# A fused cosine attention and mixer kernel: the second token mixing of odd batches cut into other bunches, one weight cast moved, the last matmul group halved

## The chip, the core and the metric

The kernel runs on one core of a Trainium2 chip. The core has five engines with their own instruction queues: TensorE (PE in the profile; PEld is its weight loading), VectorE (DVE), ScalarE (ACT), GpSimd (POOL) and SyncE (SP, which here only issues transfers). The engines work in parallel and wait for each other through semaphores. Inside one queue the order is fixed: an instruction that waits holds up everything behind it. The metric is the device time of one execution in microseconds (us), given as the median of several runs. Lower is better.

## The reference

Eight batches of twelve attention heads, each 448 positions by 64, feed a mixer block. With the names of the reference:

```python
q_n = q / (norm(q) + 1e-06);  k_n = k / (norm(k) + 1e-06)
scores = q_n @ k_n.T / tau                     # tau = 0.1
attn = softmax(scores);  x = attn @ v          # heads side by side: x is 448 x 768 for each batch
h = relu(x.T @ w_tok1) @ w_tok2                # token mixing: 448 -> 256 -> 448
u = x + h.T
h2 = relu(u @ w_ch1) @ w_ch2                   # channel mixing: 768 -> 1536 -> 768
out = u + h2
```

## The kernel before

**Attention in slots.** The 96 heads are taken two at a time: 48 pairs, six to a batch. Slot i of the main loop works on pair i and finishes pair i-1. Slots 0 to 12 run `opening`, slots 13 to 48 run `slot`. In a slot, q and k are squared on POOL (line 180), summed on DVE (`ssq`, line 190), turned into a reciprocal norm on ACT and DVE (`ln`, `nn`, `nre`, `rn`), multiplied on POOL (`qkn`, line 213) and transposed (`qkT`: on PE in the opening, by a DMA issued from SP later, line 229). `score` makes two PSUM tiles `pS` at a time (four matmuls, line 261; there are two buffers of them); ACT takes their exponentials (`pE`, line 268), two tiles at the start of a slot and two in its middle. `pv(i-1, 0)` and `pv(i-1, 1)` multiply the finished pair by v (24 and 8 matmuls in `slot`, line 282); DVE then takes a reciprocal `rec` (line 288) and writes the normalised result into the fp16 tile `x` (line 289). In `slot` the sum `ssq` for pair i+2 follows the first place for mixer jobs, so on DVE it is behind their adds; `ln` and `nn` on ACT follow it and are ahead of the slot's last two exponentials; `nre`, `rn` and the two `qkn` follow the third place.

**The mixer runs between the attention work, one batch late.** `mixer(b)` returns three lists of jobs. The token jobs: four `tok1` jobs (eight matmuls `pR`, line 313, then a ReLU on ACT, line 316) and `tok2` jobs, two for each tile of 128 tokens, one for each half of the 768 columns (four matmuls `pU`, line 326, or eight half-height ones for the shared tile 3, line 331; then a DVE add `u`, line 335). An even batch has tiles 0, 1, 2 and an odd batch tiles 3, 4, 5, 6; the odd batch's tile 3 holds the last 64 tokens of both. After the second half of a tile, the tile is cast to fp16 `u16`: odd tile numbers on DVE (line 339), even ones on ACT (line 341), and a DMA on SP transposes it into `uT` (line 342). Then twelve `ch1` jobs (six matmuls `pG`, line 379, and a ReLU on ACT, line 381), and the `ch2` jobs, two for each tile (twelve matmuls `pF`, line 388, a DVE add, line 392, and after the second half a store, line 407).

**The order.** After slot 6(b+1) the jobs of batch b are put into `todo` together with the `ch2` jobs of the batch before (`held`). Five calls of `fill` in each slot pop jobs by a credit, so that a batch's jobs spread over six slots. In `slot` the five places are: after the first two exponentials, after `pv(i-1, 0)`, after the last two exponentials, after the cast of v, and after `pv(i-1, 1)`. For an odd batch the merged list is: four `tok1`, one `ch2`, four `tok2`, one `ch2`, four `tok2`, four `ch2`, twelve `ch1`. In short names, with T for `tok2`, F for `ch2`, a number for the tile and a or b for the half:

```
tok1 x4  F0a  T3a T3b T4a T4b  F0b  T5a T5b T6a T6b  F1a F1b F2a F2b  ch1 x12
```

By the credits this list meets the slots so: batch 1 in slots 13 to 16, batch 3 in 25 to 27, batch 5 in 37 to 39. Batch 7 comes after the last slot, with no attention work left. The planner arithmetic for batches 3 and 5 (slots 25 and 26, or 37 and 38) puts F0a in the third place of the first slot, T3a T3b T4a in its fifth, T4b F0b in the first place of the next slot, T5a T5b T6a in its third and T6b F1a in its fourth.

**One ring of PSUM buffers.** All of `pT`, `pO` (of `pv`), `pR`, `pU`, `pG`, `pF` come from one pool of four buffers with one tag (`ps`). Each such tile takes the buffer of the one allocated four before it, and its first matmul waits until that one has been read, by DVE or by ACT.

**The weight cast in the opening.** `w2_cast(tt)` (line 139) casts half of the second token weight `w2t` on ACT from the staged copy `w2s`, which SP loads in the prologue (line 123). In slots 1 and 2 it stands between `norm_rec` and the second `score` (lines 495, 496), so on ACT it is ahead of the second two exponentials of its slot.

**The end.** For the last tile of the last batch (`end`) each half of the columns is stored by itself, in two pieces: one is issued from SP and the other from ACT.

`recast` (line 125) is a DVE cast written as a reduction with `max` over a length of one; the kernel has it for v and for w1.

Of the kernel before, what the change touches and what calls it, by code (L numbers as in the profile page):

```python
# [9 lines left out]
FP32 = mybir.dt.float32  # L10
FP16 = mybir.dt.float16
AF = mybir.ActivationFunctionType
ALU = mybir.AluOpType
# [10 lines left out]
def kernel(  # L24
# [19 lines left out]
    nc = tc.nc  # L44

    B, H, S, E = q.shape
    D = H * E
# [4 lines left out]
    DT, CT, TT = D // 128, C // 128, T // 128  # L52
    DH = 384
    NDH = D // DH
    NPAIR = H // 2
# [15 lines left out]
        name=nc.get_next_instruction_name(), act_func_set_id=ACT_SET_LN_EXP,  # L71
# [53 lines left out]
    def recast(out, in_):  # L125

        nc.vector.tensor_reduce(out=out, in_=bass.AP(tensor=in_.tensor, offset=in_.offset,  # L127
                                                     ap=list(in_.ap) + [[1, 1]]),
                                axis=AXX.X, op=ALU.max)
# [8 lines left out]
    def w2_cast(tt):  # L138
        nc.scalar.copy(out=w2t[:, tt, :].rearrange("k (c p) -> k c p", c=NCH),
                       in_=stage["w2"][:, tt, :].rearrange("k (p c) -> k c p", c=NCH))  # L140
# [92 lines left out]
    def tpose_pe(i, act=False, between=None):  # L233
        s = st_[i]
        s["T"] = att.tile([128, 2, S], FP16, name="qkT", tag="qkT")
        for js in ((slice(0, 1), slice(1, 2)) if act else (BOTH,)):
            pt = ps.tile([128, 2, NCH, P], FP16, name="pT", tag="ps")
            for j in range(js.start, js.stop):
                for c in range(NCH):
                    nc.tensor.transpose(pt[:, j, c, :],  # L240
                                        s["qkn"][:, j, c].rearrange("p g e -> p (g e)"),
                                        id16[:P, :P])
            o, a = s["T"][:, js].rearrange("d j s -> d (j s)"), \
                pt[:, js].rearrange("d j c p -> d (j c p)")
            if act:
                nc.scalar.copy(out=o, in_=a)
            else:
                nc.vector.tensor_copy(out=o, in_=a)  # L248
            if between and not js.start:
                between()  # L250
# [15 lines left out]
    def expo(i, c):  # L266
        s = st_[i]
        nc.scalar.activation(out=s["p"][:, c], in_=s["pS"][c][:, :, 0:S], func=AF.Exp,  # L268
                             scale=inv_tau)
# [27 lines left out]
    def mixer(b):  # L297
# [22 lines left out]
        def tok2(i, dh):  # L320
            def job():
                pU = ps.tile([128, DH], FP32, name="pU", tag="ps")
                for tt in range(TT):
                    if i != 3:
                        c0 = 128 * (i % 4)
                        nc.tensor.matmul(pU[:], w2t[:, tt, c0:c0 + 128],  # L326
                                         r16[b][:, tt, dh * DH:(dh + 1) * DH],
                                         start=(tt == 0), stop=(tt == TT - 1))
                    else:
                        for h in range(2):  # L330
                            nc.tensor.matmul(pU[64 * h:64 * h + 64], w2t[:, tt, S - 64:S],
                                             r16[2 * g + h][:, tt, dh * DH:(dh + 1) * DH],
                                             start=(tt == 0), stop=(tt == TT - 1))
                cols = slice(dh * DH, (dh + 1) * DH)
                nc.vector.tensor_tensor(out=u32[:, i - t0, cols], in0=pU[:], in1=xt[:, i, cols],  # L335
                                        op=ALU.add)
                if dh == NDH - 1:
                    if i % 2:
                        nc.vector.tensor_copy(out=u16[:, i - t0, :], in_=u32[:, i - t0, :])
                    else:  # L340
                        nc.scalar.copy(out=u16[:, i - t0, :], in_=u32[:, i - t0, :])  # L341
                    nc.sync.dma_start_transpose(
                        out=uT[:, :, (i - t0) * 128:(i - t0 + 1) * 128], in_=u16[:, i - t0, :])
            return 0.33, job
# [38 lines left out]

        def ch2(i, dh):
            def job():
                pF = ps.tile([128, DH], FP32, name="pF", tag="ps")
                for ct in range(CT):
                    nc.tensor.matmul(pF[:], gT[:, ct, (i - t0) * 128:(i - t0 + 1) * 128],  # L388
                                     wc2t[:, ct, dh * DH:(dh + 1) * DH],
                                     start=(ct == 0), stop=(ct == CT - 1))  # L390
                o = u32[:, i - t0, dh * DH:(dh + 1) * DH]
                nc.vector.tensor_tensor(out=o, in0=pF[:], in1=o, op=ALU.add)  # L392
                end = b == B - 1 and i == t0 + nt - 1
                if dh == NDH - 1 or end:
                    store(i, slice(dh * DH, (dh + 1) * DH) if end else slice(0, D), end)
            return 1.96, job

        def store(i, cols, end):
            if i == 3:
                parts = [(h, 64 * h, S - 64, 64) for h in range(2)]  # L400
            else:
                f0 = 128 * (i % 4)
                parts = [(e, f - f0, f, n) for f, n in f_segments(f0, f0 + 128)]
            for z, (h, m, f, n) in enumerate(parts):
                rows = out[2 * g + h].rearrange("(p c) d -> c p d", c=NCH)
                queue = nc.scalar if end and z else nc.sync
                queue.dma_start(out=rows[f // P, f % P:f % P + n, cols],
                                in_=u32[m:m + n, i - t0, cols])
# [9 lines left out]
    def merge(a, b):  # L418

        if not b:  # L420
            return list(a)
        r, n = [], 0
        for m, x in enumerate(b):
            while n * len(b) < (m + 1) * len(a) and n < len(a):
                r.append(a[n])
                n += 1
            r.append(x)
        return r + list(a[n:])
# [47 lines left out]
    def opening(i):  # L476

        normalize(i + 1, False)
        score(i, 0)
        norm_sum(i + 2)  # L480
        expo(i, 0)
        expo(i, 1)
        if not i:
            v_cast(0, False)
        norm_root(i + 2)
        v_cast(i + 1, i in (2, 3, 4, 5, 7))
        squares(i + 3)
        if i in wide:
            wide[i]()
        fill()  # L490
        if i >= 1:
            pv(i - 1, 0)
            pv(i - 1, 1)
        norm_rec(i + 2)
        if i in (1, 2):
            w2_cast(i - 1)
        r_, u_, add = first[0] if first else (None,) * 3
        done = [i - 2] if 2 <= i <= NPAIR else []
        if done:
            r_(i - 2)  # L500
        fill()
        score(i, 1)
        expo(i, 2)
        expo(i, 3)
        tpose_pe(i + 1)
        if i == NPAIR:
            r_(i - 1)
            done.append(i - 1)
        for pj in done:
            u_(pj)  # L510
        if i == NPAIR + 1:
            first[0][2](NPAIR - 1, False)
        for half in (True, False):
            for pj in done:
                if half or pj != NPAIR - 1:
                    add(pj, half)
        if i == NPAIR + 2:
            w1_cast(2)
        if i == 1:
            w1_cast(0)  # L520
            w1_cast(1)
        fill()
        fill()
        fill()
# [32 lines left out]
    def spread(jobs, slots):  # L557
        todo.extend(jobs)
        gap[0] = sum(c for c, _ in todo) / (5 * slots)
        credit[0] = 0.0  # L560

    for i in range(N + 1):
        if i + AHEAD < N:
            load(i + AHEAD)
        if i == 2:
            first.extend(mixer(0))
        if i < N and i % (2 * NPAIR) == 0:
            xt = mix.tile([128, 7, D], FP16, name="x16", tag="x16", bufs=2)
            x16[i // (2 * NPAIR)] = xt
            nc.vector.memset(xt[64:128, 3, :], 0.0)  # L570
        if i < FIRST:
            opening(i)
        else:
            if i == FIRST:
                normalize(i + 1, False)
                tpose_dma(i + 1)
            slot(i)
        if i == NPAIR:
            spread([(1.6, lambda: None)] + first[1][:8], NPAIR)
            late, held = first[1][8:], first[2]  # L580
        elif i and i % NPAIR == 0:
            front, c1, c2 = mixer(i // NPAIR - 1)
            spread(late + merge(front, held[:-3]) + held[-3:] + c1, NPAIR)
            late = []
            held = c2
    for _, job in todo + held:
# [36 lines left out]
```

## Time and profile before

| what | value |
|---|---|
| median of 3 runs (lowest, highest) | 408.05 us (406.93, 409.0) |
| the profiled execution's own time | 408.18 us |
| its span, first to last instruction | 406.0 us |
| ACT exponentials, line 268 | x192, 164.8 us busy, mean 913 ns |
| DVE cast of u, line 339 | x11, shortest 559, median 573, longest 1374 ns |
| ACT cast of u, line 341 | x14, 831 to 834 ns |
| DVE add after `tok2`, line 335 | x50, mean 545 ns |
| DVE `recast`, 112x512, line 127 | x40, mean 640 ns |

The profiled execution lies 0.13 us above the median of the runs, and 2.1 us of its time lie outside its span. The profile gives busy times of each engine; a busy PE is not a PE at its peak, because matmuls overlap and their ends are modelled. What one group of matmuls costs in a row of others is therefore read from the starts in the timeline: the start of the next group less its own start. The waits name for each idle stretch the instruction that ended it. The chain of waits follows the execution back from its last instruction.

### The profile page before, as it was taken

What the parts mean: (1) busy time and instruction counts of PE and PEld (TensorE: products, weight loads), DVE (VectorE), ACT (ScalarE), POOL (GpSimd) and SP (SyncE); (2) the same over time, 40 slices, a digit from 0 to 9 for tenths busy, and PEclk for the clock granted to TensorE, in tenths of its full rate; (3) what the DMA queues carried; (4) which work ended last, traced back from release to release, by engine and by line L of the source; (5) the groups of instructions that cost most, each with busy time, mean ns of one, the idle gap of its engine ahead of it and who ended that gap; (6) DMA issues with size and microseconds to landing.
All of it is one profiled execution on the core that took longest, in us unless ns stands there. A gap on an engine that the chain in (4) does not pass through costs nothing.

```text
span 406.0 us, 8998 instructions
## 1 busy us (share of the span) xinstructions
PE 382.7 (94%) x3592; PEld 219.4 (54%) x3592; DVE 234.7 (58%) x534; ACT 261.5 (64%) x451; POOL 196.2 (48%) x205
## 2 busy tenths in 40 slices
PE   2798799899999999999999999999999999999996
PEld 1465566555545555555555565555545556655453
DVE  5879978557544765467634766558644773161022
ACT  6799879865767557856687567756676665521400
POOL 3979979826544647443734655644653520000000
PEclk9999989999999999999999999999999999999999
DMA  7999999939963698529773597539972352026023
GB/s 240 260 234 213 227 293 227 242 99 190 228 135 92 160 216 203 139 79 199 225 185 101 144 189 233 131 80 191 245 157 68 78 123 84 2 61 134 0 48 109
DMA packets 97305, 63.57 MB, mean 157 GB/s; under 512 B 57520, under 2 KB 93808, under 8 KB 97264
## 3 DMA queue, kind: packets, MB, share of 16 engines
q1 hardware_dynamic: 93952, 58.14, 59.7%
q0 software_dynamic: 3184, 4.72, 6.7%
q8 instruction: 28, 0.46, 0.5%
q14 instruction: 13, 0.11, 0.1%
q10 hardware_dynamic: 128, 0.15, 0.1%
HBM read 43.38 MB, written 11.01 MB: 134 GB/s over the span
## 4 chain that ended last, share of the span: by engine, by line
PE 81%; DVE 12%; DMA 4%; ACT 2%; issue 1%; SPq 0%; DVEq 0%
PE pG L379 27%; PE pF L388 27%; PE pO L282 10%; PE pS L261 9%; PE pR L313 5%; PE pU L326 3%; DVE ssq L190 2%; DVE x L289 2%; DMA kl<-in_k_dram 1%; DVE qkT L248 1%; DVE u L370 1%; ACT pE L268 1%; DMA ql<-in_q_dram 1%; DMA w2s<-in_moe_w_tok_dram 1%; DVE u L335 1%; DVE rec L288 1%
## 5 line engine op out<-in xcount | busy, mean ns | idle before, releaser
L268 ACT ACTIVATE pE<-pS 112x896 f16<-112x896 f32 x192 | 164.8, 913 | 35.3 <-PE pS L261 34.7
L379 PE MATMUL pG<-uT,wc1t 128*128 128x384 f16 (+1 forms) x576 | 121.4, 355 | 0.0
L388 PE MATMUL pF<-wc2t,gT 128*128 128x384 f16 x672 | 116.6, 326 | 0.2
L213 POOL TENSOR_TENSOR qkn<-ql,rn 112x512 f16<-112x512 f32 x47 | 49.0, 1043 | 130.6 <-DVE rn L202 109.6
L388 PEld LDWEIGHTS <-gT 128*128 128x128 f16 x672 | 63.5, 98 | 47.0 <-issue 7.3
L381 ACT ACTIVATE gT<-pG 128x384 f16<-128x384 f32 (+1 forms) x96 | 52.4, 547 | 44.8 <-PE pG L379 43.9
L379 PEld LDWEIGHTS <-wc1t 128*128 128x128 f16 x576 | 51.6, 98 | 51.4 <-issue 11.0
L392 DVE TENSOR_TENSOR u<-pF,u 128x384 f32<-128x384 f32 x56 | 31.1, 555 | 78.0 <-PE pF L388 77.7
L261 PE MATMUL pS<-qkT 64*112 64x448 f16 x384 | 60.3, 385 | 9.8 <-DVE qkT L248 5.1
L282 PEld LDWEIGHTS <-pE 112*128 112x128 f16 x1536 | 59.0, 99 | 16.1 <-issue 5.6
L282 PE MATMUL pO<-v,pE 112*128 112x65 f16 x1536 | 62.8, 196 | 0.0
L288 DVE RECIPROCAL rec<-pO 128x6 f32<-128x6 f32 x96 | 17.5, 182 | 76.1 <-PE pO L282 75.2
L190 DVE TENSOR_REDUCE ssq<-sq 112x16 f32<-112x1024 f32 (+1 forms) x50 | 58.5, 1171 | 4.2 <-ACT sq L178 3.1
L180 POOL TENSOR_TENSOR sq<-ql 112x512 f32<-112x512 f32 x46 | 48.7, 1058 | 5.6 <-DMA ql<-in_q_dram 5.6
L213 POOL TENSOR_TENSOR qkn<-kl,rn 112x512 f16<-112x512 f32 x47 | 49.0, 1042 | 0.0
L180 POOL TENSOR_TENSOR sq<-kl 112x512 f32<-112x512 f32 x46 | 48.3, 1051 | 0.0
L289 DVE TENSOR_TENSOR x<-pO,rec 128x384 f16<-128x384 f32 x96 | 40.9, 426 | 3.3
L261 PEld LDWEIGHTS <-qkT 64*112 64x112 f16 x384 | 19.1, 128 | 35.6 <-issue 22.6
L127 DVE TENSOR_REDUCE v<-vl 112x512 f16<-112x512 f32 x40 | 25.5, 640 | 0.0
L335 DVE TENSOR_TENSOR u<-pU,x 128x384 f32<-128x384 f32 x50 | 25.4, 545 | 0.1
L341 ACT CAST u<-u 128x768 f16<-128x768 f32 x14 | 11.6, 832 | 20.9 <-DVE u L335 20.9
L194 ACT ACTIVATE ln<-ssq 112x16 f32<-112x16 f32 (+1 forms) x49 | 10.9, 222 | 17.5 <-DVE ssq L190 17.2
(43 smaller groups left out, 183.4 us busy)
## 6 DMA issues: line engine op xcount, KB each, us to landing
ql<-in_q_dram SPq DMA_DIRECT2D x48, 224.0 KB, 3.6
kl<-in_k_dram SPq DMA_DIRECT2D x48, 224.0 KB, 4.0
vl<-in_v_dram SPq DMA_DIRECT2D x48, 224.0 KB, 4.2
out_dram<-u SPq DMA_DIRECT2D x8, 336.0 KB, 3.4
wc1t<-in_moe_w_ch_dram POOLq DMA_DIRECT2D x4, 576.0 KB, 7.9
wc2t<-in_moe_w_ch_dram POOLq DMA_DIRECT2D x3, 768.0 KB, 10.1
out_dram<-u SPq DMA_DIRECT2D x8, 288.0 KB, 3.8
out_dram<-u SPq DMA_DIRECT2D x7, 240.0 KB, 3.0
```

Of the source, the lines that this page charges most:

```text
L180: nc.gpsimd.tensor_mul(out=s["sq"][:, j], in0=a, in1=a)
L190: nc.vector.tensor_reduce(out=small(i, "ssq")[:, j], in_=st_[i]["sq"][:, j], axis=AXX.X, op=ALU.add)
L213: eng.tensor_tensor(out=t[:, j].rearrange("p c g e -> p g c e"), in0=s[nm][:], in1=_bcast_free(rn, E), op=ALU.mult)
L261: nc.tensor.matmul(pS[:, h, 0:S], s["T"][64 * h:64 * h + 64, 1, c * P:(c + 1) * P], s["T"][64 * h:64 * h + 64, 0, :], start=True, stop=True)
L268: nc.scalar.activation(out=s["p"][:, c], in_=s["pS"][c][:, :, 0:S], func=AF.Exp, scale=inv_tau)
L282: nc.tensor.matmul(pO[:, n, h, :], s["p"][:, c, h, c0:c0 + 128], s["v16"][:, NCH * h + c, 0:E + 1], start=(c == 0), stop=(c == NCH - 1))
L289: nc.vector.tensor_tensor(out=xt[hp:hp + nr, t0:t0 + len(ts), d0:d0 + 2 * E].rearrange("p t (h e) -> p t h e", h=2), in0=pO[m0:128, :, :, ...
L335: nc.vector.tensor_tensor(out=u32[:, i - t0, cols], in0=pU[:], in1=xt[:, i, cols], op=ALU.add)
L379: nc.tensor.matmul(pG[:], wc1t[:, dt, ct * 128:(ct + 1) * 128], uT[:, dt, :], start=(dt == 0), stop=(dt == DT - 1))
L381: nc.scalar.activation(out=gT[:, ct, :], in_=pG[:], func=AF.Relu)
L388: nc.tensor.matmul(pF[:], gT[:, ct, (i - t0) * 128:(i - t0 + 1) * 128], wc2t[:, ct, dh * DH:(dh + 1) * DH], start=(ct == 0), stop=(ct == C ...
L392: nc.vector.tensor_tensor(out=o, in0=pF[:], in1=o, op=ALU.add)
```

## The change

Four edits in one diff.

1. For odd batches the merged list is written out by hand: four `tok1`, T3a T3b, F0a, T4a T4b T5a, F0b, T5b T6a T6b, then the same four `ch2` and the `ch1`. Even batches keep the merge.
2. The casts to `u16`: tiles 1 and 5 stay on DVE, but as `recast`; tile 3 goes to ACT with the even tiles.
3. `w2_cast(0)` in slot 1 stands after the slot's last two exponentials; `w2_cast(1)` in slot 2 stays.
4. The very last `ch2` group (second half of the last tile of batch 7) is done as two groups of 192 columns, each with its own twelve matmuls, add and two stores.

```diff
@@ tok2
                 if dh == NDH - 1:
-                    if i % 2:
-                        nc.vector.tensor_copy(out=u16[:, i - t0, :], in_=u32[:, i - t0, :])
+                    if i in (1, 5):
+                        recast(u16[:, i - t0, :], u32[:, i - t0, :])
                     else:
                         nc.scalar.copy(out=u16[:, i - t0, :], in_=u32[:, i - t0, :])
@@ ch2
-                pF = ps.tile([128, DH], FP32, name="pF", tag="ps")
-                for ct in range(CT):
-                    nc.tensor.matmul(pF[:], gT[:, ct, (i - t0) * 128:(i - t0 + 1) * 128],
-                                     wc2t[:, ct, dh * DH:(dh + 1) * DH],
-                                     start=(ct == 0), stop=(ct == CT - 1))
-                o = u32[:, i - t0, dh * DH:(dh + 1) * DH]
-                nc.vector.tensor_tensor(out=o, in0=pF[:], in1=o, op=ALU.add)
                 end = b == B - 1 and i == t0 + nt - 1
-                if dh == NDH - 1 or end:
-                    store(i, slice(dh * DH, (dh + 1) * DH) if end else slice(0, D), end)
+                parts = 2 if end and dh == NDH - 1 else 1
+                for z in range(parts):
+                    cols = slice(dh * DH + z * DH // parts, dh * DH + (z + 1) * DH // parts)
+                    pF = ps.tile([128, DH // parts], FP32, name="pF", tag="ps")
+                    for ct in range(CT):
+                        nc.tensor.matmul(pF[:], gT[:, ct, (i - t0) * 128:(i - t0 + 1) * 128],
+                                         wc2t[:, ct, cols],
+                                         start=(ct == 0), stop=(ct == CT - 1))
+                    o = u32[:, i - t0, cols]
+                    nc.vector.tensor_tensor(out=o, in0=pF[:], in1=o, op=ALU.add)
+                    if end:
+                        store(i, cols, end)
+                if dh == NDH - 1 and not end:
+                    store(i, slice(0, D), end)
@@ opening
-        if i in (1, 2):
-            w2_cast(i - 1)
+        if i == 2:
+            w2_cast(1)
...
         expo(i, 3)
+        if i == 1:
+            w2_cast(0)
         tpose_pe(i + 1)
@@ main loop
-            spread(late + merge(front, held[:-3]) + held[-3:] + c1, NPAIR)
+            if (i // NPAIR) % 2:
+                mid = merge(front, held[:-3]) + held[-3:]
+            else:
+                mid = front[:6] + held[:1] + front[6:9] + held[1:2] + front[9:] + held[2:]
+            spread(late + mid + c1, NPAIR)
```

By the credits the new list meets slots 25 and 26 (and 37 and 38) so: T3a T3b in the third place of the first slot, F0a in its fourth, T4a in its fifth; T4b T5a F0b in the first place of the next slot, T5b T6a in its third, T6b F1a in its fourth. For batch 1, slot 14 takes T3a T3b F0a, T4a T4b, T5a F0b and T5b in its first, third, fourth and fifth place, and slot 15 begins with T6a T6b F1a in both versions.

## The prediction

> **What bounds the kernel now.** I read the page's busy shares first, then busy time by stage, then the timeline of the stages in which PE is not full, the chain of waits in the opening, and last the end of the span.
>
> ```profile
> PE 382.7 (94%) x3592; PEld 219.4 (54%) x3592; DVE 234.7 (58%) x534; ACT 261.5 (64%) x451; POOL 196.2 (48%) x205
> ```
>
> PE is the fullest engine, but it is not full everywhere. By stage (busy us of each engine in the stretch, granted clock, DMA):
>
> ```profile
> 150.00:170.00 20.00, 20.00 (x204) 11.81 (x203) 11.84 (x28) 14.18 (x28) 11.69 (x12) 1.00 0.75 186
> 170.00:195.00 25.00, 24.11 (x230) 13.98 (x226) 16.50 (x37) 15.29 (x26) 9.89 (x11) 1.00 0.65 148
> 195.00:218.00 23.00, 23.00 (x200) 11.03 (x199) 11.04 (x28) 17.61 (x31) 15.07 (x15) 1.00 0.66 174
> ```
>
> From 80 us on PE is busy without a break except in two stretches, 170 to 195 and 262 to 288: slots 25 to 27 and 37 to 39, the token mixing of batches 3 and 5. So time saved on PE there reaches the end, since nothing after it waits for anything but PE. In the timeline of slot 26 (start, duration, engine, instruction):
>
> ```profile
> 178.15 0.29 DVE L289 TENSOR_TENSOR x<-pO,rec 64x128 f16<-64x128 f32 x1
> 178.48 1.02 DVE L335 TENSOR_TENSOR u<-pU,x 128x384 f32<-128x384 f32 x2
> 178.50 0.50 PE L326 MATMUL pU<-r,w2t 128*128 128x384 f16 x2
> 179.09 2.11 PE L388 MATMUL pF<-wc2t,gT 128*128 128x384 f16 x12
> 179.53 1.37 DVE L339 CAST u<-u 128x768 f16<-128x768 f32 x1
> 180.45 1.35 POOL L180 TENSOR_TENSOR sq<-kl 112x512 f32<-112x512 f32 x1
> 182.22 1.20 DVE L190 TENSOR_REDUCE ssq<-sq 112x16 f32<-112x1024 f32 x1
> 183.56 0.56 DVE L289 TENSOR_TENSOR x<-pO,rec 128x384 f16<-128x384 f32 x1
> 184.18 0.50 PE L326 MATMUL pU<-r,w2t 128*128 128x384 f16 x2 [0.65 <-DVE x L289]
> 184.64 2.11 PE L388 MATMUL pF<-wc2t,gT 128*128 128x384 f16 x12
> ```
>
> The last T6b (184.18) needs the buffer of the pO whose `x` ends at 184.12; that `x` is behind `ssq`, which is behind the adds and a cast of 1.37 us. PE pays by the ring of four buffers.
>
> In the opening, the chain of waits (start, duration, work):
>
> ```profile
> 13.53 3.95 DMA w2s<-in_moe_w_tok_dram
> 17.48 0.02 issue
> 17.51 0.99 ACT w2t L139
> 18.50 1.64 ACT pE L268 x2
> 20.13 0.04 issue
> 20.18 0.62 PE pS L261 x2
> 20.80 1.88 PE pO L282 x32
> ```
>
> ACT stands before `w2_cast(0)` until w2s has landed (17.48), with slot 1's last two exponentials behind it.
>
> **Unit prices**, from start to start: two `score` tiles 0.52 (173.75 to 174.27); a half of tile 3 0.385 (two from 176.57 to 177.34); any other `tok2` 0.325 (four from 361.59 to 362.89); a `ch2` 1.95; `pv` 0.82 (181.04 to 181.86) and 0.34 (176.23 to 176.57).
>
> **Edit 1, batches 3 and 5.** Where PE loses time before, by the ring: T4b begins at 178.50, though the scores in front end at 177.77 + 0.52 = 178.29 (0.21, waiting for `x`); F0b at 179.09 against 178.83 (0.26, T3a's add); T6b at 184.18 against 182.38 + 3 x 0.325 = 183.36 (0.82); F1a at 184.64 against 184.51 (0.13). Sum 1.42 us. The new order from 173.75: scores 0.52, T3a T3b 0.77, F0a 1.95, `pv` 0.34, T4a 0.33, scores 0.52, T4b T5a 0.65, F0b 1.95, `pv` 0.82, scores 0.52, T5b T6a T6b 0.98: 9.35, so F1a could start at 183.10. Does DVE keep up? T3's adds run from about 174.8 to 175.8, in idle DVE time (3.08 us stand in front of 176.43 now). T4b, T5a, F0b take buffers of T3b, F0a and the small pO, read by 178.3, when they are asked for at 178.28, 178.60 and 178.93. F0b ends at 180.87; its add to 181.55, `ssq` (1.13 by the chain) to 182.7, `rec` and `x` to 183.4. F1a takes that pO's buffer: it starts at about 183.45, 0.35 late instead of 1.42 or more. Against 184.64 that is 1.15 us a batch once small gaps are let stand, **2.3 us for two**. Ends: 0 if a new wait of the same length arises, 1.42 x 2 = 2.84 if all goes. After F1a the same work follows with no gap now (184.64 to `ch1` at 195.51 is 10.87 by the trace, 10.85 by the prices). The queues must follow. On SP, T3's transpose now stands ahead of `qkT` and the next three loads instead of behind `qkT`: it waits for ACT's cast to about 176.8, while `qkT` waits for POOL to about 178.3 anyway, so it delays nothing. T6's transpose, issued at 190.61 now, moves up about 1.4 us with `rn` and `qkn`; median landing 3.9 us, so about 193.1, before `ch1` at 194.4.
>
> **Batch 1.** Between 83.23 and F1a at 92.92 its gaps are only some 0.3 us, and the new order makes F0b wait for `x` (T3's adds, F0a's add and `ssq` come first): 0.05 gained, ends -0.3 and +0.3. **Batch 7**: PE has no gap from 353 to 402. T3b now follows the `tok1` group directly and needs its last ReLU, which ends at 356.86; the second half of T3b would start at 356.75: **+0.15**, ends 0 and 0.5 (one ReLU, 0.49).
>
> **Edit 2, casts.** Off DVE: tile 3's four (0.56, 1.37, 1.37, 0.56). Seven become `recast`. No row has 128x768 alone: the nearest are 0.64 for 512 columns and 1.17 for `ssq` over 1024; in proportion 0.92 (ends 0.64, 1.17). Tile 5's four go from 0.57 to 0.92, tile 1's three from 1.03 (that is what 139.85 shows, beside a POOL square of 1.35) to 0.92. On PE's path this is already in the DVE times above; in slots 20, 32, 44 PE has no gap and DVE idles 0.65 before 137.41 and 1.17 before 129.34, so 0. If that cover were gone: 4 x 0.35 = 1.4. ACT gets four casts of 0.83. From 170 to 195 ACT is busy 15.29 of 25 us; behind T4's cast stand `ln`, `nn` and two exponentials, needed by the `pv` of slot 27 at about 188.3, ready at 184.8. Behind T3's cast stand slot 26's first exponentials, but it is done at 176.8, and their scores at 178.2. So 0; uncovered, 4 x 0.83 = 3.3.
>
> The casts and a rule that speaks against them: "VectorE: DVE Perf Modes" in the Trainium skill ("Rules for kernel authors", and its tier table) has `tensor_reduce` at 1x only, as the slowest Vector operation, and an fp32 copy at 2x. The undisturbed casts (0.57) against 0.64 for a third fewer columns agree with it. By that rule alone the change would lose about 7 x 0.35 = 2.5 us where DVE is the limit (an estimate: 407.6 in place of 405.1); I don't follow it because the casts that hurt lasted 1.37 and 1.03.
>
> **Edit 3.** The second two exponentials of slot 1 can start when their scores are ready: PE starts them at 16.56, the first pair takes 0.66 to reach ACT (13.76 to 14.42), so 17.22 instead of 18.50 in the chain. Then w2_cast, 18.9 to 19.85. Slot 2's scores are then bound by `qkT` (ends 19.07) instead of by the exponentials: 19.13 to 20.1, and `pO` starts at 20.1 instead of 20.73. Slot 2's first exponentials start at 19.85, and 1.72 + `ln`, `nn`, v cast, second w2 cast follow on ACT nearly as now (that chain gains only 0.15 to 0.3, but before 24.11 and 26.48 ACT idles 0.17 and 0.64 now, so it has room). By slot 3 the gain is between 0.15 (ACT) and 0.63 (PE). From there to 49 us the chain is DVE work end on end, with POOL and ACT nearly as full, and moves as a whole: **0.5**, nearer PE's bound since ACT has that room. w2t's first reader is in slot 2, after both casts.
>
> **Edit 4.**
>
> ```profile
> 402.03 0.56 DVE L392 TENSOR_TENSOR u<-pF,u 128x384 f32<-128x384 f32 x1 [1.32 <-PE pF L388]
> 402.62 0.32 SPq L407 DMA_DIRECT2D out_dram<-u  x1
> 402.62 0.38 ACTq L407 DMA_DIRECT2D out_dram<-u  x1
> ```
>
> 192 columns lie between the adds of 128 (0.29) and 384 (0.56): 0.36, gain 0.2. Its transfer halves from 192 KB, but stores of 48 KB take 3.0 us to land and of 120 KB 2.0, so size gains between 0 and 0.4: 0.2. Twice as many weight loads: 128 columns run at 0.054 us each with their loads (line 351, eight in 0.61 with the last one's delay), 192 need 0.08, so 0. The first half's two issues are through 0.6 us earlier. **0.4**, ends -0.4 (two issues more in the way) and 0.6.
>
> **Sum** against the profiled execution's own 408.18: -2.3 - 0.05 + 0.15 - 0.5 - 0.4 = -3.1, **405.1 us**. The median of the runs, 408.05, is 0.13 lower and within their spread, so I leave it.
>
> **Rivals.**
> A, the sum: 405.1, own range 404.0 to 406.0; **0.57**. For it: the ring, applied to the old order, gives each of the four waits to within 0.06 us.
> B, the waits move: `x` behind `ssq` again holds the ring in slots 26 and 38 so that half of the 2.3 stays, and ACT's chain limits the opening to 0.15: 408.18 - 1.15 - 0.05 + 0.15 - 0.15 - 0.2 = 406.8; **0.26**. For it: the number of buffers is unchanged, and the four `ch2` behind the last bunch were already four. Against: T3's adds come 3.7 us earlier (174.8 for 178.48).
> C, slower: ACT's queue. Tile 3's cast makes three of four tiles there; if the copies hold exponentials that PE then waits for, four casts of 0.83 and tile 5's 4 x 0.35 show, the ring's gain is lost, and 408.18 + 3.3 + 1.4 + 0.15 - 0.9 = 412.1. It decides once ACT is more than 3.5 us late (184.8 against 188.3). Against: the idle times above; **0.07**.
> D, better: the PE clock. In the rows of single microseconds the granted clock is 0.50 from 50 to 53, after an idle PE at 48; matmuls there take twice as long (six `pG` 2.04 against 0.98). If the shifted opening misses that stretch, up to 1.7 more goes: 403.4; **0.10**.
>
> On D, "TensorE: Matmul & The Clock Gate" (Part 1, "What's actually happening") says that the gate looks at free-running windows of about 3.4 us; the stretch here is as long as one. By it a second such window would cost as much as the first, and where it falls is chance.
>
> About 0.5%, 2.0 us, is what a measurement can tell from no change: below 406.0 is faster. A without its upper edge and D give **0.66**, B and that edge **0.27**, C **0.07**. Range **403.3 to 407.6**: D's time at the bottom; at the top the sum without any of the ring's gain and with half the tail's (408.18 - 0.05 + 0.15 - 0.5 - 0.2 = 407.6). C is left out.
>
> **What would show it.** PE's waits for `x` (1.3 us on L326) gone, F1a about 9.7 us after 173.75's scores instead of 10.9; L339 gone; the first `pE` of slot 1's second half at about 17.2 and `pO` 0.6 earlier; a last add of 0.36. Wrong would be: new PE waits at L388 for L289 in these slots as long as the old ones, or exponentials ended late by L341.

## The result and the profile after

| | before | changed |
|---|---|---|
| median of 12 runs each | 408.44 us | 405.05 us |
| ratio changed/before, 95% interval | | 0.9905 [0.9878, 0.9933] |
| the profiled execution's own time, its span | 408.18, 406.0 us | 405.19, 403.1 us |

The ratio is that of the means of the compared runs: the kernel became faster by 3.9 us (2.7 to 5.0 by the interval, of 408.44), while the two medians differ by 3.4. The forecast was 3.1 less, 405.1, and lies inside that interval. The two profiled executions differ by 3.0. Runs more than 1.5% above the fastest of their kernel are left out of the ratios and of the runs called compared below: one here (409.75 us at a clock of 0.983), seven of 48 over the five series that have edit 3 and no extra matmuls, and none of the 113 of the series without edit 3, before among them.

The busy shares on the changed kernel's page:

```profile
PE 381.0 (95%) x3604; PEld 219.3 (54%) x3604; DVE 232.9 (58%) x531; ACT 264.0 (65%) x455; POOL 194.6 (48%) x205
```

And its windows around the mixing of batch 3 (window, length, busy us and instructions of PE, PEld, DVE, ACT and POOL, then the granted clock, DMA share and GB/s):

```profile
150.00:170.00 20.00, 20.00 (x205) 11.77 (x203) 11.91 (x28) 14.25 (x28) 11.76 (x12) 1.00 0.79 188
170.00:195.00 25.00, 24.85 (x236) 14.50 (x233) 16.80 (x39) 16.69 (x29) 10.77 (x12) 1.00 0.69 164
195.00:218.00 23.00, 23.00 (x206) 11.29 (x205) 10.92 (x25) 18.04 (x33) 13.81 (x14) 1.00 0.62 163
```

In the stretch 170 to 195 PE is now busy 24.85 us of 25 (24.11 before). ACT is busy 16.69 there (15.29 before) and DVE 16.80 (16.50); over the whole span ACT took on 2.5 us and DVE gave up 1.8. The first scores of slot 25 before, from which the stage is counted:

```profile
169.80 0.59 PE L261 MATMUL pS<-qkT 64*112 64x448 f16 x4
```

The timeline of slots 25 and 26 in the changed kernel:

```profile
169.73 0.59 PE L261 MATMUL pS<-qkT 64*112 64x448 f16 x4
...
174.76 1.02 DVE L335 TENSOR_TENSOR u<-pU,x 128x384 f32<-128x384 f32 x2 [1.48 <-PE pU L331]
...
175.81 0.83 ACT L341 CAST u<-u 128x768 f16<-128x768 f32 x1
...
178.25 1.49 DVE L335 TENSOR_TENSOR u<-pU,x 128x384 f32<-128x384 f32 x3
...
181.40 1.21 DVE L190 TENSOR_REDUCE ssq<-sq 112x16 f32<-112x1024 f32 x1
...
182.07 1.15 PE L326 MATMUL pU<-r,w2t 128*128 128x384 f16 x6
...
182.75 0.56 DVE L289 TENSOR_TENSOR x<-pO,rec 128x384 f16<-128x384 f32 x1
...
183.36 2.12 PE L392 MATMUL pF<-wc2t,gT 128*128 128x384 f16 x12
183.80 0.95 DVE L127 TENSOR_REDUCE u<-u 128x768 f16<-128x768 f32 x1
```

Tile 3's adds run at 174.76, right behind their matmuls. `ssq` starts at 181.40 instead of 182.22, the three last `tok2` run without a break from 182.07, and only F1a still waits: 182.07 + 3 x 0.325 = 183.05, it starts at 183.36, just after the `x` that began at 182.75. From the first scores of slot 25 to F1a it is 183.36 - 169.73 = 13.63 us; before it was 184.64 - 169.80 = 14.84. For batch 5 the same two numbers come out.

The end:

```profile
398.76 0.36 DVE L396 TENSOR_TENSOR u<-pF,u 128x192 f32<-128x192 f32 x1 [0.36 <-PE pF L392]
...
399.15 1.30 SPq L412 DMA_DIRECT2D out_dram<-u  x2
...
399.75 0.36 DVE L396 TENSOR_TENSOR u<-pF,u 128x192 f32<-128x192 f32 x1 [0.63 <-PE pF L392]
```

The last add takes 0.36 instead of 0.56 us, and from its end to the end of the span it is 3.0 us instead of 3.45.

Where the time came from is read by setting the timelines side by side: for each slot, the start of its first scores less the start of the first PE instruction, as a difference to the profiled execution of before (negative is earlier). The columns stand for the kernels of the experiments below; "end" is the end of the span.

```
slot    changed  order  casts    w2   half   no w2  changed, again  no casts
   8      -0.20  -0.72  -0.81  -1.25  -0.64  -0.62           -1.49     -1.12
   9      -0.19  -2.26  -1.67  -2.14  -0.63  -0.78           -3.03     -2.66
  25      -0.22  -2.28  -1.70  -1.88  -0.46  -0.81           -2.79     -2.49
  27      -1.41  -3.47  -2.20  -1.88  -0.45  -2.00           -3.99     -3.68
  39      -2.59  -4.66  -2.70  -1.87  -0.45  -3.19           -5.18     -4.87
  47      -2.59  -4.66  -2.70  -1.87  -0.44  -3.19           -5.17     -4.87
 end      -3.07  -4.53  -2.66  -1.85  -0.99  -3.62           -5.63     -5.31
```

Two things are to be seen. From slot 9 on the columns are flat to within 0.3 us but for the steps at 27 and 39, where batches 3 and 5 mix their tokens, and for the end: what is gained there is kept. And at slot 9 the columns differ by 2.8 us even where two kernels are the same (the first and the last but one). Half of that arises between slots 8 and 9: the columns "changed", "half" and "no w2", whose profiles have the clock at 0.50 around 50 us as before has, gain nothing there (0.2 at most), and the other five, which have no such stretch, gain 0.9 to 1.5 us.

### The profile page after: what moved, and what is told of

Read it like the earlier page. It is cut to its first block, busy times and chain, and to the rows that moved or that the text cites. A ratio compares the mean times of both kernels' runs of the same rounds, so it can differ in the third digit from the quotient of the medians.

```text
span 403.1 us, 9030 instructions
## 1 busy us (share of the span) xinstructions
PE 381.0 (95%) x3604; PEld 219.3 (54%) x3604; DVE 232.9 (58%) x531; ACT 264.0 (65%) x455; POOL 194.6 (48%) x205
## 4 chain that ended last, share of the span: by engine, by line
PE 84%; DVE 10%; ACT 4%; issue 1%; DMA 1%
PE pF L392 28%; PE pG L379 27%; PE pO L282 10%; PE pS L261 10%; PE pR L313 5%; DVE ssq L190 3%; PE pU L326 3%; ACT pE L268 2%; DVE x L289 2%; DVE qkT L248 1%; DVE u L370 1%; PE pU L331 1%; DMA ql<-in_q_dram 1%; DVE rec L288 1%; DVE u L396 1%
## 5 line engine op out<-in xcount | busy, mean ns | idle before, releaser
L392 PE MATMUL pF<-wc2t,gT 128*128 128x384 f16 (+1 forms) x684 | 116.7, 324 | 0.4
L396 DVE TENSOR_TENSOR u<-pF,u 128x384 f32<-128x384 f32 (+1 forms) x57 | 31.3, 550 | 69.2 <-PE pF L392 69.1
L180 POOL TENSOR_TENSOR sq<-ql 112x512 f32<-112x512 f32 x46 | 47.8, 1039 | 6.1 <-DVE ssq L190 6.1
L341 ACT CAST u<-u 128x768 f16<-128x768 f32 x18 | 15.0, 832 | 15.7 <-DVE u L335 15.7
```

The source lines that it names most:

```text
L180: nc.gpsimd.tensor_mul(out=s["sq"][:, j], in0=a, in1=a)
```

## The experiments

Each ran in five rounds beside the kernel of before on the same chip.

**The order alone** (`e1_order`): of the change only

```diff
...
+            else:
+                mid = front[:6] + held[:1] + front[6:9] + held[1:2] + front[9:] + held[2:]
...
```

> The new order of the odd batches' jobs alone; tiles 1, 3 and 5 are still cast by the DVE copy of before. Theory R (the ring: the order brings tile 3's adds into idle DVE time, and with them frees the buffers in time): nearly all of the stage's gain without the casts, F1a of batch 3 about 13.6 to 13.8 us after the first scores of slot 25 (14.84 before, 13.63 in the changed kernel), 2.2 to 2.4 us less in all. Rival K (the long DVE copies are the cause, the order is secondary): 14.3 us or more there, at most 1 us less in all.

Ratio 0.9926 [0.9894, 0.9958]. From slot 25's first scores to F1a 13.63 us (167.90 to 181.53), the changed kernel's number exactly, with the DVE copies in place; the two steps in the table are 1.19 each. Tile 3's copy, brought into idle DVE time, takes 0.56 us and not 1.37. At the end it loses 0.13: T3b waits for a ReLU. Theory R holds, K falls.

**The casts alone** (`e2_casts`):

```diff
-                    if i % 2:
-                        nc.vector.tensor_copy(...)
+                    if i in (1, 5):
+                        recast(u16[:, i - t0, :], u32[:, i - t0, :])
```

> The casts alone (tiles 1 and 5 as recast, tile 3 on ACT), old order. Theory R: only the 1.37 us copies go; x before T6b ends about 0.6 earlier and T5a's add then holds F1a, so 14.84 becomes about 14.2 in slot 25, 1.2 us less in all for batches 3 and 5; the waits of T4b and F0b (0.21, 0.26) stay. Rival K: 13.7 or less, 2.2 us less in all. Rival C (ACT's queue): no gain or a loss.

Ratio 0.9954 [0.9931, 0.9976]. 168.37 to 182.70, 14.33 us: 0.51 a batch. T4b and F0b still wait; `ssq` moves up and T6b with it. So about two fifths of the gain (0.51 of 1.21) could have been had either way, and the order takes all of what the casts would give. Of the 1.9 us by the runs the two batches are 1.0; by its profile the rest lies before slot 9, where profiles of one kernel differ as well. Theory R holds in size; rival K, which asked for 2.2 us, falls, and so does C, which asked for no gain.

**The casts of before in the changed kernel** (`e12_no_casts`):

```diff
-                    if i in (1, 5):
-                        recast(u16[:, i - t0, :], u32[:, i - t0, :])
+                    if i % 2:
+                        nc.vector.tensor_copy(out=u16[:, i - t0, :], in_=u32[:, i - t0, :])
```

> The changed kernel with the casts of before (tiles 1, 3, 5 by the DVE copy): order, w2 move and halved group alone. Theory R (the order is the whole of the stage's gain): 13.63 us from slot 25's first scores to F1a, the changed kernel's time at the same clock within 0.3. Rival: the DVE copies cost 0.5 a batch or more, 1 us in all.

Ratio 0.9899 [0.9861, 0.9938], 13.63 us from 167.71 to 181.34. Its runs at a granted clock of 0.998 or more have a median of 402.5, the changed kernel's 402.8 and 402.6. Edit 2 adds nothing that shows once the order is there. The comparison is at full clock; over all its compared runs the kernel has 402.4 to 407.5 us.

**All casts on ACT** (`e8_all_act`):

```diff
-                    if i in (1, 5):
-                        recast(u16[:, i - t0, :], u32[:, i - t0, :])
-                    else:
-                        nc.scalar.copy(out=u16[:, i - t0, :], in_=u32[:, i - t0, :])
+                    nc.scalar.copy(out=u16[:, i - t0, :], in_=u32[:, i - t0, :])
```

> The changed kernel with all casts to u16 on ACT (tiles 1 and 5 too). Rival C of the prediction (ACT's queue becomes the limit): F1a of batch 3 later than 13.63 us after slot 25's first scores, or waits for pE in slots 26 and 27, 1 us or more in all. Theory R: ACT has room, 13.5 to 13.63 there and the same time within 0.3 us at the same clock.

Ratio 0.9877 [0.9837, 0.9917]; its runs at full clock have a median of 402.35. In its profiled execution too F1a of batch 3 comes 13.63 us after the first scores of slot 25 (175.79 to 189.42). Rival C of the prediction falls: even seven more casts of 0.83 us than in the changed kernel cost nothing.

**The w2 cast alone** (`e3_w2`):

```diff
-        if i in (1, 2):
-            w2_cast(i - 1)
+        if i == 2:
+            w2_cast(1)
...
         expo(i, 3)
+        if i == 1:
+            w2_cast(0)
```

> The w2 cast moved, alone. Theory P (the chain of waits in the opening moves as a whole): 0.5 us less, whichever windows of the PE clock are at half rate. Theory G (the gate decides): the profiled opening up to slot 8 is not shorter by more than 0.2 where a half-rate window has moved into 26 to 29.5 us, and over the runs the time goes with the granted clock: runs at 1.0 about 2 us below runs at 0.992, so that the median changes by which of them is more frequent, -2 to +1.

Ratio 0.9975 [0.9947, 1.0002]: 1.0 us, not separated from nothing. Its profiled execution and that of the order alone can be compared: in both the first record of a full clock stands near 24 us (23.8 and 24.1), and it holds to the end of the work. There the move is worth 1.25 - 0.72 = 0.53 us at slots 4 to 8, as theory P says; the changed kernel with the old casts, whose clock became full at the same time as that of the order alone, has 1.12 - 0.72 = 0.40, the changed kernel's second execution, where it did so 0.9 us sooner, 0.77. But in slot 9 the lead is gone (2.14 against 2.26). The timeline of `e3_w2` shows a wait there:

```profile
48.53 0.63 PE L261 MATMUL pS<-qkT 64*112 64x448 f16 x4 [1.59 <-DVE qkT L248]
49.10 0.82 PE L379 MATMUL pG<-uT,wc1t 128*128 128x384 f16 x4
50.27 0.61 PE L379 MATMUL pG<-uT,wc1t 128*128 128x384 f16 x2 [0.35 <-DMA uT<-u]
```

The first channel mixing group is reached before the last transposed piece of `uT` has landed. In the changed kernel's two profiles no such wait stands there, so it is no fixed price. Of theory G the split by the clock shows in the runs: those at 0.998 or more have a median of 406.0 us and those below it 408.25. The half-rate window at 26 us that it takes for the profile does not stand there.

**The changed kernel again, and without the w2 move** (`e9_changed`, `e6_no_w2`; the second undoes the diff of `e3_w2`):

> The changed kernel again, as the partner of the three below. Ratio to before about 0.9905 again; by the granted clock its runs fall into two heaps, about 402.7 at 1.0 and about 405 at 0.992.

> The changed kernel without the move of the w2 cast. Theory U (the 0.5 that the move gains by slot 8 is taken back there by the first channel mixing group, which then waits for the last transposed uT): same time as the changed kernel at the same clock, within 0.3; where no half-rate window falls behind 24 us, slot 9's scores at the same time after the first PE instruction. Theory P (the gain goes through): 0.5 more.

`e9_changed`: 0.9901 [0.9865, 0.9937]. Its compared runs are 402.3, 402.6, 402.7 at a clock of 1.0, 403.5 at 0.996, 404.6, 405.1 at 0.992 and 405.8 at 0.987 (the eighth run took 411.3 at 0.979); the first series has 402.5, 402.7, 402.9 and 403.9 at 1.0 and 404.7 to 405.9 below. Two heaps, as expected. `e6_no_w2`: 0.9929 [0.9902, 0.9956], 1.1 us behind in the middle, with overlapping intervals. Below full clock the two agree (medians 404.94 and 404.85, of eleven runs and four), as theory U has it; but the wait for `uT` that U gives as the reason does not stand in the changed kernel's profiles, and its lead of 0.77 over the order alone is still there in slot 9 (3.03 against 2.26). At full clock the one run without the move took 403.3, those with it 402.3 to 402.7, as theory P has it. Between the two this does not decide. What differs more is how often the clock is full: one run of twelve without the move has 0.998 or more, and three of seven with it. (A mean of 0.998 leaves no room for a stretch of 3.4 us at half clock, which takes 0.004 off a span of 405 us.) Over all these kernels without extra matmuls: with the w2 move 22 of 41 compared runs have 0.998 or more (22 of all 48), without it 15 of 113; of the two pairs that differ in the move alone, `e3_w2` has 6 of 11 against 3 of 32 of before on the same chip, and the changed kernel 3 of 7 against 1 of 12. So runs without a fall of the clock go with the move; how it brings them about no run shows.

**The last group alone** (`e4_last`; its edit is the `ch2` part of the diff):

> The last group halved, alone. By the trace of the changed kernel: the last add begins 0.16 earlier after the last group's start and takes 0.36 for 0.56, and the end comes 3.0 for 3.45 us after the last add: 0.6 us less. Rival (two more stores in the way): no change or 0.4 more.

Ratio 0.9994 [0.997, 1.0018]: too small for the runs. In the table it goes from -0.44 to -0.99, 0.55 us at the end; this rests on one profile.

**Extra matmuls to hold the clock.** First in front of the scores (`e7_warm`; 40 before the first transpose, then these):

```diff
             pS = pss.tile([P, 2, 512], FP32, name="pS", tag="pS")
+            for _ in range(WARM.get((i, c), 0)):
+                nc.tensor.matmul(pS[:, 0, 0:128], id16[:, :P], id16[:], start=True, stop=True)
```

> The changed kernel plus matmuls on the identity whose results are overwritten: 40 before the first transpose, 8 in front of the first scores of slots 3 to 7, 24 in slot 8, 4 in slot 9, all where PE waits. Theory G (the run to run spread and much of the opening's time is the PE clock at half rate): no half-rate window between the first full one and the end, full rate before 18 us, runs within 1 us of each other at a clock of 1.0, median 401.5 to 403. Rival (the opening is set by DVE and ACT, the clock only goes with it): median 405 as the changed kernel, or more by the matmuls' own 1 us.

0.991 [0.9878, 0.9942], median 404.45, eight runs from 403.9 to 405.1. Theory G is right on the spread and on the profile (full clock from 17.4 us and no fall after it), and wrong on the time, 401.5 to 403; four of the eight runs have a clock of 0.982 or 0.983 and yet the same time. The low heap went too: the extra matmuls wait for the `pS` buffers and push each slot's scores back (24.71 to 29.41, 4.70 us a slot where 4.44 was). So I put them where PE has nothing to wait for but the next `qkT`, into a buffer of their own: at the end of slot 7 (`e10_gap7`, `GAP = {7: 24}`), and in slots 2 to 7 with the 40 at the start and the casts of `e8_all_act` (`e11_gaps`):

```diff
+        if GAP.get(i, 0):
+            pW = ps.tile([128, 128], FP32, name="pW", tag="ps")
+            for _ in range(GAP[i]):
+                nc.tensor.matmul(pW[:], id16[:], id16[:], start=True, stop=True)
         if i == 1:
             w1_cast(0)
```

> The changed kernel plus 24 matmuls on the identity at the end of slot 7, into a buffer of their own that nobody reads, where PE stands 1.6 us for the qkT of slot 8. Theory G (the half-rate window around 50 us comes of that idle stretch): no half-rate window between 48 and 53 us, fewer runs at 0.992 or less, median 0.5 to 1.5 below the changed kernel's 404 to 405. Rival (the window comes of the whole opening's thin use of PE): windows there as often as before.

> The same, with 40 before the first transpose, 4 to 8 at the ends of slots 2 to 6 and 24 in slot 7, and all casts on ACT. Theory G: no half-rate window behind the first full one, all runs at 402 to 403.5. Rival (the extra matmuls push the scores back, as the ones in front of the scores did with 0.27 a slot): slot pitch above 4.44 us in slots 4 to 7 and 404 or more.

The timeline of `e10_gap7` in slots 7 and 8:

```profile
46.37 0.57 PE L241 MATMUL pT<-id,qkn 112*128 112x112 f16 x8
46.83 1.51 PE L530 MATMUL pW<-id 128*128 128x128 f16 x24
48.52 0.63 PE L262 MATMUL pS<-qkT 64*112 64x448 f16 x4 [0.18 <-DVE qkT L249]
```

The idle stretch of 1.59 us is 0.18 now. `e10_gap7`: 0.9894 [0.9862, 0.9926], median 402.94; four of five compared runs lie between 402.6 and 403.1, one at 405.2 (the sixth run took 412.3 at 0.983). `e11_gaps`: 0.9889 [0.9862, 0.9915], median 402.97, all six runs between 402.3 and 404.2, one of them above the forecast 403.5; from slot 4 to slot 8 its scores take 18.9 us as before has (20.3 in `e7_warm`), so the rival falls. By their intervals neither is separated from the changed kernel's 0.9905 and 0.9901, nor from the lowest ratio of the study, 0.9877 of `e8_all_act`; by their runs they mostly stay in the low heap, and `e11_gaps` is the only kernel of the study with no run above 404.2. These runs alone do not settle that the window around 50 us is caused by the idle stretch of slot 8: the changed kernel's second execution had the stretch and no window. The last section reads it from the traces.

## Why the prediction was right

**What bounds the kernel.** Right: a microsecond taken from PE in slots 25 to 27 or 37 to 39 is there at the end; the table shows it unchanged from one step to the next. That the sum of 3.1 met 3.0 in the profiled pair so closely is in part luck: there the opening gave 0.2 of the 0.5, and the two batches and the end a little more than their terms, and the two executions have their stretches at half clock in different places.

**Edit 1, batches 3 and 5** (2.3 us): 1.21 a batch by F1a, 2.4 in all. The step by step working holds too: F1a was to wait 0.35 for `x` and waits 0.31. The ring of four buffers, the adds behind `ssq` and the earlier adds of tile 3 are the mechanism: the order alone gives all of it, and no wait of PE on line 326 for `x` is left. **Batch 1** (0.05): from slot 14's first scores to F1a 83.23 to 92.92 before and 83.19 to 92.88 now, 9.69 both times, 0. **Batch 7** (+0.15): +0.13.

**Edit 2** (0): right as a sum. `recast` of 768 columns takes 0.95 us (0.92 was taken). Alone it gives 0.5 a batch, because it moves up `ssq`; I had counted it inside the DVE times of edit 1 and not said that the order doesn't need it. The rule on `tensor_reduce` as the slow operation in "VectorE: DVE Perf Modes" of the Trainium skill ("Rules for kernel authors") agrees in the duration (0.95 against 0.56 for the undisturbed copy), and costs nothing here, since DVE is not what PE waits for at that place.

**Edit 3** (0.5): the mechanism right, the term taken too simply. The second exponentials of slot 1 start at 17.39 in the changed kernel (17.2 was forecast), and in its second execution `pO` of slot 2 starts 0.67 us sooner after the first PE instruction than before (0.6 was forecast). Where the clock became full at about the same time the move gives 0.40 to 0.53 by slot 8; in the recorded pair of profiles only 0.2 is left. The windows of both (busy us, granted clock and DMA at the end of a row), first before, then changed:

```profile
20.00:24.00 4.00, 3.82 (x46) 2.96 (x45) 2.94 (x8) 3.86 (x8) 2.93 (x3) 1.00 1.12 286
26.00:29.00 3.00, 2.97 (x56) 2.31 (x57) 2.93 (x6) 2.49 (x5) 3.00 (x4) 1.00 0.74 174
```

```profile
20.00:24.00 4.00, 2.80 (x57) 2.22 (x54) 3.73 (x10) 3.97 (x8) 3.84 (x5) 1.00 1.10 306
26.00:29.00 3.00, 3.00 (x44) 2.57 (x41) 1.96 (x7) 2.15 (x6) 2.20 (x3) 0.50 1.28 255
```

The 1.00 of the first row is not a measured full clock: the views count the time ahead of the trace's first record of the clock as full, and that record stands at 26.1 us before and at 18.7 us in the changed kernel. The matmuls show it. The same 32 take, before and then changed:

```profile
20.73 1.94 PE L282 MATMUL pO<-v,pE 112*128 112x65 f16 x32
26.56 1.15 PE L282 MATMUL pO<-v,pE 112*128 112x65 f16 x32
```

```profile
19.81 1.15 PE L282 MATMUL pO<-v,pE 112*128 112x65 f16 x32
```

So in the changed kernel PE runs slot 2 at full clock and in less time, is busy only 2.80 of 4 us, and then falls to a clock of 0.50 between 26 and 29 us, when before has just become full. In slot 4 the gain of 1.6 us that it had in slot 3 is down to 0.2. The term took no account of the clock in the opening, which shifts the result by more than its own 0.5.

**Edit 4** (0.4): 0.55, the add 0.2 and the shorter way to the end 0.45, less what the two parts take.

**The rivals.** B and C are ruled out: the waits did not move, and ACT had room for more casts. (B's 0.15 for the opening is near the 0.2 of the recorded pair, but there the clock took the rest back, and not ACT.) D had a chance of 0.10 at 403.4: it is the low heap at 402.7, and 4 of the 11 compared runs are in it. Missing the stretch around 50 us is worth 0.9 to 1.5 us in the table (D took up to 1.7). I saw the stretch at half clock in the profile but held it for rare chance; the spread of the three runs, 406.93 to 409.0, was a sign of it. Whether it lies behind the difference between 3.1 and the 3.9 measured is not shown, since 3.1 is inside the interval. The low heap does weigh more: 9 of the 68 runs of before in the later series have 0.998 or more, 7 of the 18 compared runs of the changed kernel. Why that goes with the w2 move is open.

## What to carry to other kernels

Where PE waits for a ring of buffers, follow the ring: which reader frees the buffer four allocations back, and what stands ahead of that reader on its engine. Starting the reader's work earlier, in time that is idle anyway, can be worth more than making it shorter. And where runs of one kernel spread by 2 us, look first at the granted clock of each run and at where in the trace it changes: two kernels are compared at the same clock, and here it fell where PE's idle time came to lie within one window.

## What the runs showed of the hardware

The clock of PE falls to 0.50 for 3.4 us at a time (25.6 to 29.0 and 49.5 to 52.9 us in the profiled execution of the changed kernel), though PE stood idle for no longer than 1.6 us at a stretch before. "TensorE: Matmul & The Clock Gate" in the Trainium skill (Part 1, "What's actually happening") gives the window of about 3.4 us, which agrees, and names an idle window as the cause, which these traces don't show.

What they show is a share. Between the first record and the end of the work, the stretches at full or half clock in all 13 profiles last whole multiples of 3.41 us (3.41, 6.83, 10.24, 20.48, 23.89 and so on). Cut into windows of that length on each profile's own changes, PE was busy 1.43 to 1.97 us in the ten windows at full clock that a fall followed, and 2.00 us or more in the 1401 that none followed (up to the last 3 us of its work). The gap between the two is thin, and some matmul records can be missing. The rows of five windows, each with the kernel that it is of:

```profile
46.05:49.46 3.41, 1.60 (x25) 0.96 (x22) 3.21 (x9) 3.25 (x7) 3.23 (x4) 1.00 1.01 181
```

(the changed kernel, before the fall at 49.5)

```profile
45.13:48.54 3.41, 1.97 (x37) 1.32 (x33) 3.21 (x9) 3.25 (x7) 3.22 (x5) 1.00 1.14 222
```

(`e6_no_w2`, before a fall: the busiest of the ten)

```profile
20.81:24.23 3.42, 2.00 (x27) 1.36 (x24) 2.73 (x8) 3.39 (x8) 2.67 (x4) 1.00 1.13 258
```

(`e7_warm`, no fall: the least busy of the others)

```profile
43.69:47.10 3.41, 2.72 (x48) 1.74 (x46) 3.28 (x8) 2.98 (x6) 3.41 (x5) 1.00 1.38 248
47.10:50.52 3.42, 2.29 (x35) 1.64 (x36) 3.19 (x6) 3.14 (x5) 3.23 (x4) 1.00 0.98 171
```

(the changed kernel's second execution, no fall)

The last two rows answer the question of the idle stretch in slot 8. It is 1.59 us long in both executions of the changed kernel; in the first, one window holds all of it, and in the second a boundary at 47.10 us leaves part of it on each side. The 24 matmuls of `e10_gap7` lift the two windows there to 3.19 and 3.23 us, and the clock holds. Where the boundaries lie differs between these two executions of one kernel. That this is what puts its runs into heaps is likely; only the profiled executions show their boundaries.

In the changed kernel two such windows go with about 2.3 us (405.1 against 402.8). The mean clock of a run is no sure guide: three runs of before at 1.0 took 407.05, 408.83 and 409.56 us. It counts the time ahead of the first record as full, and half clock behind the last work as lost: in the profiled execution of before, (3.41 + 1.07) x 0.5 us lost of 406.0 give its 0.994, and the 26.1 us ahead of the first record take nothing off.
